# First loads and first products of an attention and MLP-mixer kernel put in another order

## The chip, the cores and the metric

The kernel runs on one core of a Trainium2 chip. The core has a matrix engine (TensorE, PE in the profile), a vector engine (VectorE, DVE), a scalar engine (ScalarE, ACT), a general engine (GpSimd, POOL) and a sync engine (SyncE, SP). Each runs its own list of instructions in order, and they wait for each other by semaphores. SP, ACT and POOL also issue DMAs, which 16 DMA engines carry out. The metric is the device time of one execution in microseconds (us), smaller being better.

## What is computed

Eight batches of attention with eight heads, with no softmax but a division by the root mean square, and then an MLP mixer on the result:

```
kv  = einsum('bhsd,bhse->bhde', k, v)             # 8 x 8 heads, seq 576, head_dim 64
o   = einsum('bhsd,bhde->bhse', q, kv)
x   = o / sqrt(mean(o*o, -1) + 1e-6) * g_norm     # heads side by side: (8, 576, 512)
h   = relu(x.transpose(0,2,1) @ w_tok1) @ w_tok2  # token mixing, 576 -> 256 -> 576
u   = x + h.transpose(0,2,1)
out = u + relu(u @ w_ch1) @ w_ch2                 # channel mixing, 512 -> 1536 -> 512
```

Everything is float32. The weights reach the chip as 64-bit words and are turned into float32 on ACT and DVE.

## The kernel before

**Tiles.** The 576 rows of a batch are cut into 4 tiles of 128 rows (512 rows, `LO`) and a remainder of 64 rows (`HF`). k and v of a batch lie in tiles `k_in`, `v_in` of 128 partitions by 5 slots of 512: slots 0 to 3 hold the main rows (4 consecutive rows to a partition, 1024 KB in all) and slot 4 holds the remainder in partitions 0 to 63 (128 KB), the other half being zero. There are two such tiles each, for the even and the odd batch. q of a batch comes transposed, as 128 partitions by 4 head pairs by 512 rows (`qT`, 1024 KB), and its last 64 rows in a tile of their own (`qR`).

**Pairs.** Two batches are worked together as a pair, so that the two remainders fill one tile. A pair has nine x tiles: 0 to 3 of its first batch (side 0), 4 to 7 of its second (side 1), and 8 with both remainders. `attention` numbers them by c (0 to 4) and half: c = 0, 1 are the first batch, c = 2, 3 the second, c = 4 the remainders.

**Stages.** In the first 187 us attention and token mixing of four pairs are interleaved on PE; channel mixing follows until the end. The change lies in the first pair's stage, which takes about the first 40 us.

**Order.** The order of work on each engine is the order of the program text, because every instruction is recorded with `keep_in_program_order`. The interleaving of a stage is written out by hand as a list of short names, which `play` calls one after the other. The list for the first pair is `start` (line 1297). In it, with s for a side or batch, c for a pair of x tiles and t for a half:

- `kv s half`: the products of k and v of a batch, for half of its heads, into the PSUM tile `ps_kv` (line 371). For each block it adds up over slots j = 0 to 4, so the remainder is the last term. `e s half` copies the result to `kvp`: on DVE for side 0 of the first pair, else on ACT (line 385).
- `a c t`: q times `kvp` for one x tile, into a PSUM bank `ps_o`, of which there are two (line 393). `a40` is the remainder tile, shown as `ps_r`.
- `q c t`: the square on ACT (L455); `g c t`: times `g_norm` on DVE, which writes the x tile (L451); `t c t`: the sum of squares on DVE (L472); `m`, `r`, `i`: mean (DVE), root (ACT), inverse (DVE, four instructions). Only when both `q` and `g` have read a bank can the next `a` but one use it.
- `d c t`: the x tile scaled by the inverse on DVE, one instruction (L509). `s c t`: the same on ACT, eight instructions of 64 columns (L505).
- `h s t j`: token mixing of x tile j of side s with half t of `w_tok1`, into `ps_h` (line 539); x tiles 0 and 1 use the first block of weights, 2 and 3 the second.
- `w n k`: step k of weight block n (1 and 2 on ACT and DVE: scale; clamp, shift, add). `w0*` and `w1*` are the two blocks of `w_tok1`, `w2*` its remainder, `w3*` and `w4*` `w_tok2`.
- `l`, `lq`, `lr`: loads of k and v, q, and q's remainder, for the batch two further on.
- `j n`: n products of the identity with itself, for a PE that would else stand still.

**Loads ahead of the list.** Lines 1275 to 1283 issue: k and v of batch 0 (k on SP's queue, v on ACT's), q of batch 0, the two blocks of `w_tok1`, k and v of batch 1, q of batch 1, both remainders of q, and the remainder of `w_tok1`. All but v of batch 0 go through SP. ACT then issues `g_sb`, the 64 values of `g_norm` sent to 128 partitions in rows of 256 bytes. The loads use eight semaphores in turn, so each issue first waits until the DMA eight places back has landed.

Of the kernel before, what the change touches and what calls it, by code (L numbers as in the profile page):

```python
# [11 lines left out]
F32 = mybir.dt.float32  # L12
# [8 lines left out]
def kernel(  # L21
# [33 lines left out]
    P = 128  # L55
# [5 lines left out]
    J, JJ, HF = 4, 5, 64  # L61
    LO = P * J
    assert D == 64 and DM == 512 and S == LO + HF and B % 2 == 0
    NC, NF, NTOK = DM // P, DCH // P, DTOK // P
    HP = H // 2
# [7 lines left out]
    T = 2 * P  # L73
# [4 lines left out]
    def pool(name, bufs, side="left", stack=ctx, **kw):  # L78
        return stack.enter_context(tc.tile_pool(name=name, bufs=bufs, side=side,
                                                reuse_waits="tile", **kw))  # L80
# [10 lines left out]
    qtp = pool("qtp", 2, "left", left)  # L91
# [30 lines left out]
    def dma(o, i, engine=nc.sync):  # L122
        keep(engine.dma_start(o, i))  # L123
# [14 lines left out]
    qT, q_rest = {}, {}  # L138

    def load(b):  # L140

        if b >= B:
            return

        queues = (nc.sync, nc.sync if b else nc.scalar)
        for dst, t, e in zip((k_in[b % 2], v_in[b % 2]), (k, v), queues):
            dma(dst[:, :J], t[b, :LO].rearrange("(p j) e -> p j e", j=J), e)
            dma(dst[:HF, J], t[b, LO:], e)

    def load_q(b):  # L150
        if b < B:
            qT[b] = qtp.tile([P, HP, LO], F32, name="qT", tag="qT", bufs=2)
            dma(qT[b], q[b].rearrange("(c p) s -> p c s", p=P)[..., :LO])

    def load_q_rest(b):
        if b < B:
# [57 lines left out]
    def get_tok1(i):  # L214

        rows = words(moe_w_tok1)[:LO].rearrange("(i j p) n w -> i p j n w", j=2, p=P)
        return block(2 * DTOK, lambda raw: [(raw.rearrange("p (j n) w -> p j n w", j=2), rows[i])], w_tok1[i])

    def get_tok1_rem():
        w = words(moe_w_tok1)[LO:]  # L220
        return block(DTOK, lambda raw: [(raw[:HF], w), (raw[HF:], w)], w_tok1r)
# [139 lines left out]
    def attention(pair, groups):  # L361
# [154 lines left out]
        for s in range(2):  # L516
            for h in range(2):
                steps |= {f"kv{s}{h}": do(kv, s, h), f"e{s}{h}": do(evict, s, h),
                          f"l{s}": do(load, 2 * pair + 2 + s)}
            steps |= {f"lq{s}": do(load_q, 2 * pair + 2 + s), f"lr{s}": do(load_q_rest, 2 * pair + 2 + s)}  # L520
# [735 lines left out]
    def play(lines, after={}, **stages):  # L1256
# [3 lines left out]
        for name in " ".join(lines).split():  # L1260
# [5 lines left out]
            else:  # L1266
# [4 lines left out]
    tok1 = [get_tok1(i) for i in range(J // 2)] + [get_tok1_rem()]  # L1271
    tok2 = [get_tok2(t) for t in range(NTOK)]
    channel = ([get_ch1(c, f) for f in range(2) for c in range(NC)]
               + [get_ch2(f) for f in range(NF // 2)])
    load(0)
    load_q(0)
    for block in tok1[:2]:
        block[0]()
    load(1)
    load_q(1)  # L1280
    load_q_rest(0)
    load_q_rest(1)
# [4 lines left out]
    for t in zeroed:  # L1287
# [8 lines left out]

    start = [
        "j14 kv00 e00", "kv01 e01 l0", "a00 g00 q00", "a01 g01 q01 t00 t01 m0 w01",
        "a10 w02 r0 i0 w03 d00 w04 d01 q10 w30 w40 lq0", "a11 q11 g10 g11 w11 j10",
        "h000 h010 w12 w13 w14 t10 t11 m1 r1", "h001 h011", "kv10 e10", "kv11 e11 i1 d10 d11 l1", "a20 q20",  # L1300
        "a21 q21 g20 g21 t20 t21 m2", "h002 h012 r2 i2 d20", "a30 q30 g30", "a31 q31 s21 g31 t30", "h003 h013 t31 m3",
        "a40 q40 r3 i3 d30 s31 g40 t40 m4 r4 w21 i4 s40 lr0 lr1"]
    middle = [
        "h100 h110 h101 h111 w31 w22 w23 w24", "kv00 e00 -lq1 w32 w33 w34",
# [156 lines left out]
```

## Time and profile before

| what | us |
|---|---|
| device time, median of 3 runs (lowest, highest) | 773.03 (772.90, 773.72) |
| device time of the profiled execution | 774.16 |
| its span, first to last instruction | 772.3 |
| PE busy | 761.5 |
| DVE busy | 642.8 |
| ACT busy | 277.5 |

Device time includes 1.9 us around the span. Busy time is what an engine spent in instructions. A timeline row gives start, length, engine, line, operation, output and inputs, number of instructions, and in brackets how long the engine stood idle before it and what released it. On PE every float32 product shows as two records. All products are recorded in one helper (line 135), so rows are told apart by the tile they write. SP's timeline around the first loads:

```profile
0.74 1.01 SPq L123 DMA_DIRECT2D k_in<-in_k_dram  x2
1.80 1.01 SPq L123 DMA_DIRECT2D qT<-in_q_dram  x1
2.86 1.25 SPq L123 DMA_DIRECT2D raw<-in_moe_w_tok_dram  x2
9.08 1.04 SPq L123 DMA_DIRECT2D k_in<-in_k_dram  x2
10.56 0.86 SPq L123 DMA_DIRECT2D v_in<-in_v_dram  x2
13.68 0.38 SPq L123 DMA_DIRECT2D qT<-in_q_dram  x1
```

Here the gap between 4.1 and 9.08 is the wait for a semaphore of the eight: the first MB of v landed at 9.04.

### The profile page before, as it was taken

What the parts mean: (1) busy time and instruction counts of PE and PEld (TensorE: products, weight loads), DVE (VectorE), ACT (ScalarE), POOL (GpSimd) and SP (SyncE); (2) the same over time, 40 slices, a digit from 0 to 9 for tenths busy, and PEclk for the clock granted to TensorE, in tenths of its full rate; (3) what the DMA queues carried; (4) which work ended last, traced back from release to release, by engine and by line L of the source; (5) the groups of instructions that cost most, each with busy time, mean ns of one, the idle gap of its engine ahead of it and who ended that gap; (6) DMA issues with size and microseconds to landing.
All of it is one profiled execution on the core that took longest, in us unless ns stands there. A gap on an engine that the chain in (4) does not pass through costs nothing.

```text
span 772.3 us, 12663 instructions
## 1 busy us (share of the span) xinstructions
PE 761.5 (99%) x4682; PEld 613.5 (79%) x4682; DVE 642.8 (83%) x945; ACT 277.5 (36%) x555; POOL 112.1 (15%) x124
## 2 busy tenths in 40 slices
PE   7999999999999999999999999999999999999998
PEld 6655555545888888888888888888888888888887
DVE  2867887897776868989978889987998997798996
ACT  2376575765210233521134252223352224325221
POOL 1002021113410000002240001042000218000204
PEclk9999999999999999999999999999999999999999
DMA  8999999499799696598898577999659879955679
GB/s 309 323 343 362 372 374 359 174 289 346 245 279 357 258 300 188 167 279 184 232 228 266 148 215 230 249 192 266 197 159 281 174 217 208 207 150 152 150 203 119
DMA packets 137819, 188.29 MB, mean 244 GB/s; under 512 B 48800, under 2 KB 95392, under 8 KB 135712
## 3 DMA queue, kind: packets, MB, share of 16 engines
q1 hardware_dynamic: 101744, 167.54, 69.1%
q0 software_dynamic: 34816, 18.36, 16.0%
q10 hardware_dynamic: 1200, 1.61, 0.6%
q8 instruction: 37, 0.61, 0.3%
q14 instruction: 22, 0.18, 0.1%
HBM read 138.31 MB, written 49.15 MB: 243 GB/s over the span
## 4 chain that ended last, share of the span: by engine, by line
PE 95%; DMA 3%; DVE 1%; SPq 0%; ACT 0%; issue 0%; ACTq 0%
PE ps_d L135 28%; PE ps_b L135 19%; PE ps_a L135 19%; PE ps_u L135 8%; PE ps_h L135 7%; PE ps_v L135 5%; DMA qT<-in_q_dram 3%; PE ps_c L135 3%; PE ps_w L135 2%; PE ps_o L135 2%; PE ps_kv L135 2%; PE ps_r L135 0%; DVE x L451 0%; DVE ms L472 0%; SPq L123 0%
## 5 line engine op out<-in xcount | busy, mean ns | idle before, releaser
L135 PE MATMUL ps_d<-ui,w 128*128 128x256 f32 x504 | 118.6, 379 | 0.0
L135 PEld LDWEIGHTS ps_d<-ui,w 128*128 128x128 f32 x504 | 95.8, 190 | 13.0
L132 ACT COPY ps_d<-ps_a 128x768 f32<-128x768 f32 (+1 forms) x56 | 32.0, 572 | 199.9 <-PE ps_a L135 196.9
L126 DVE TENSOR_TENSOR v<-v,v 128x1536 f32<-128x1536 f32 (+2 forms) x70 | 103.3, 1483 | 0.3
L135 PE MATMUL ps_b<-sv,w 128*128 128x256 f32 x324 | 78.9, 379 | 0.0
L135 PE MATMUL ps_a<-v,w 128*128 128x256 f32 x324 | 78.8, 379 | 0.0
L1205 POOL DMA_DIRECT2D out_dram<-us x24 | 26.7, 1834 | 291.9 <-ACT p L132 286.2
L135 PEld LDWEIGHTS ps_b<-sv,w 128*128 128x128 f32 x324 | 61.2, 190 | 8.9 <-issue 0.6
L135 PEld LDWEIGHTS ps_a<-v,w 128*128 128x128 f32 x324 | 61.6, 190 | 8.4
L135 PE MATMUL ps_u<-h,w_tok 128*128 128x512 f32 (+1 forms) x160 | 64.7, 599 | 0.0
L135 PE MATMUL ps_d<-v,w 128*128 128x256 f32 x258 | 62.7, 379 | 0.0
L129 ACT ACTIVATE v<-v 128x768 f32<-128x768 f32 (+1 forms) x54 | 42.7, 822 | 55.1 <-DVE v L126 53.4
L135 PE MATMUL ps_h<-x,w_tok 128*128 128x512 f32 x128 | 57.4, 599 | 0.3 <-DVE w_tok L188 0.3
L1205 POOL DMA_DIRECT2D out_dram<-r x40 | 41.3, 1927 | 102.0 <-ACT p L132 80.3
L135 PE MATMUL ps_d<-sv,w 128*128 128x256 f32 x228 | 55.4, 379 | 0.0
L135 PEld LDWEIGHTS ps_d<-v,w 128*128 128x128 f32 x258 | 48.9, 190 | 6.6
L135 PEld LDWEIGHTS ps_u<-h,w_tok 128*128 128x128 f32 (+1 forms) x160 | 25.6, 179 | 31.1 <-issue 26.7
L135 PEld LDWEIGHTS ps_d<-sv,w 128*128 128x128 f32 x228 | 43.3, 190 | 5.9
L135 PE MATMUL ps_a<-uT,w 128*128 128x256 f32 x192 | 46.7, 379 | 0.0
L135 PEld LDWEIGHTS ps_h<-x,w_tok 128*128 128x128 f32 x128 | 23.5, 190 | 27.7 <-issue 25.0
L135 PE MATMUL ps_b<-ui,w 128*128 128x256 f32 x168 | 40.8, 379 | 0.0
L135 PEld LDWEIGHTS ps_a<-uT,w 128*128 128x128 f32 x192 | 36.5, 190 | 5.0
(165 smaller groups left out, 1292.4 us busy)
## 6 DMA issues: line engine op xcount, KB each, us to landing
w<-parts SPq DMA_DIRECT2D x168, 384.0 KB, 3.8
w<-parts SPq DMA_DIRECT2D x56, 192.0 KB, 3.8
uT<-blocks SPq DMA_DIRECT2D x36, 256.0 KB, 5.5
k_in<-in_k_dram SPq DMA_DIRECT2D x8, 1024.0 KB, 12.2
qT<-in_q_dram SPq DMA_DIRECT2D x8, 1024.0 KB, 12.6
out_dram<-x POOLq DMA_DIRECT2D x16, 512.0 KB, 8.0
v_in<-in_v_dram SPq DMA_DIRECT2D x7, 1024.0 KB, 15.8
raw<-in_moe_w_ch_dram SPq DMA_DIRECT2D x8, 768.0 KB, 11.5
```

What stands on the lines that cost most here:

```text
L126: keep(engine.tensor_tensor(out=o, in0=a, in1=b, op=op))
L129: keep(nc.scalar.activation(o, a, AF.Relu))
L132: keep(nc.scalar.copy(o, a))
L135: keep(nc.tensor.matmul(*a, **kw))
L1205: keep(nc.gpsimd.dma_start(to, t()[ds(b * Q, Q), at].rearrange("p n l j -> p n (l j)"), accum_op=ALU.add))
```

## The change

There are four edits. In `load`, the remainder of k and of v is issued ahead of the main rows, for every batch. `load_q` can load a range of q's rows, and batch 0's q is loaded as rows 0 to 255, then the first block of `w_tok1`, then rows 256 to 511, then the second block; later batches load q whole as before. In `start`, x tile 1 (c = 0, half 1) is scaled by ACT (`s01`, after `q11`) where DVE did it (`d01`). And PE's order in the second half of `start` is another: `h002 h012` stand ahead of `a20 a21` instead of behind them, and `h003 h013` ahead of `a30 a31`; the steps of the inverse move along in the list. The numbers of instructions on PE and POOL stay the same; DVE has one less, ACT eight more, and SP one more DMA.

```diff
         queues = (nc.sync, nc.sync if b else nc.scalar)
         for dst, t, e in zip((k_in[b % 2], v_in[b % 2]), (k, v), queues):
+            dma(dst[:HF, J], t[b, LO:], e)
             dma(dst[:, :J], t[b, :LO].rearrange("(p j) e -> p j e", j=J), e)
-            dma(dst[:HF, J], t[b, LO:], e)
-
-    def load_q(b):
+
+    def load_q(b, at=slice(0, LO)):
         if b < B:
-            qT[b] = qtp.tile([P, HP, LO], F32, name="qT", tag="qT", bufs=2)
-            dma(qT[b], q[b].rearrange("(c p) s -> p c s", p=P)[..., :LO])
+            if at.start == 0:
+                qT[b] = qtp.tile([P, HP, LO], F32, name="qT", tag="qT", bufs=2)
+            dma(qT[b][..., at], q[b].rearrange("(c p) s -> p c s", p=P)[..., at])
...
     load(0)
-    load_q(0)
-    for block in tok1[:2]:
+    for i, block in enumerate(tok1[:2]):
+        load_q(0, slice(i * T, i * T + T))
         block[0]()
     load(1)
...
     start = [
         "j14 kv00 e00", "kv01 e01 l0", "a00 g00 q00", "a01 g01 q01 t00 t01 m0 w01",
-        "a10 w02 r0 i0 w03 d00 w04 d01 q10 w30 w40 lq0", "a11 q11 g10 g11 w11 j10",
-        "h000 h010 w12 w13 w14 t10 t11 m1 r1", "h001 h011", "kv10 e10", "kv11 e11 i1 d10 d11 l1", "a20 q20",
-        "a21 q21 g20 g21 t20 t21 m2", "h002 h012 r2 i2 d20", "a30 q30 g30", "a31 q31 s21 g31 t30", "h003 h013 t31 m3",
+        "a10 w02 r0 i0 w03 d00 w04 q10 w30 w40 lq0", "a11 q11 s01 g10 g11 w11 j10",
+        "h000 h010 w12 w13 w14 t10 t11 m1 r1", "h001 h011", "kv10 e10", "kv11 e11 i1 d10 d11 l1", "h002 h012",
+        "a20 q20", "a21 q21 g20 g21 t20 t21 m2", "h003 h013 r2 i2 d20", "a30 q30 g30", "a31 q31 s21 g31 t30 t31 m3",
         "a40 q40 r3 i3 d30 s31 g40 t40 m4 r4 w21 i4 s40 lr0 lr1"]
```

## The prediction

> **What bounds the kernel now.** I read the page first (busy shares), then PE's waits, then PE's timeline of the first 45 us, the chain of waits for the same stretch, the DMA issues one by one, and the windows of the DMA dip near 9 us.
>
> ```profile
> PE 761.5 (99%) x4682; PEld 613.5 (79%) x4682; DVE 642.8 (83%) x945; ACT 277.5 (36%) x555; POOL 112.1 (15%) x124
> PE ps_j L135 <- POOL ident masks.py:199: 3.3, 1, 3.3
> PE ps_o L135 <- DMA qT<-in_q_dram: 2.2, 2, 1.1
> PE ps_o L135 <- ACT sq L455: 0.5, 1, 0.5
> PE ps_kv L135 <- DMA v_in<-in_v_dram: 0.4, 1, 0.4
> PE ps_h L135 <- DVE w_tok L188: 0.3, 1, 0.3
> PE ps_r L135 <- DVE x L451: 0.2, 1, 0.2
> ```
>
> These are all the waits that PE has in the whole execution (total, times, longest, in us). They all lie before 36 us. From there to its last matmul PE never waits, so whatever moves `a40` (the ps_r matmuls) moves the end by as much. Apart from the fixed 3.3 us at the start, 3.7 us of waiting is all that a reordering of this stage could remove, and a later `a40` is lost in full.
>
> ```profile
> 13.80 2.02 PE L135 MATMUL ps_o<-kvp,qT 128*128 128x128 f32 x16 [1.12 <-DMA qT<-in_q_dram]
> 20.95 3.70 PE L135 MATMUL ps_h<-x,w_tok 128*128 128x512 f32 x8 [0.32 <-DVE w_tok L188]
> 24.61 2.76 PE L135 MATMUL ps_kv<-v_in,k_in 128*64 128x64 f32 x80
> 28.47 2.02 PE L135 MATMUL ps_o<-kvp,qT 128*128 128x128 f32 x16 [1.10 <-DMA qT<-in_q_dram]
> 30.33 1.88 PE L135 MATMUL ps_h<-x,w_tok 128*128 128x512 f32 x4
> 35.93 1.09 PE L135 MATMUL ps_r<-kvp,qR 128*64 128x128 f32 x16 [0.22 <-DVE x L451]
> ```
>
> These rows of PE's timeline (start, length) are `a00`/`a01`; `h000` to `h011`; `kv10`/`kv11`; `a20`/`a21`; `h002`/`h012`; `a40`. The row without a wait, 24.61, matters most: it shows none, yet it has hardly any slack:
>
> ```profile
> v_in<-in_v_dram SPq DMA_DIRECT2D x1, 1024.0 KB, 13.9
> v_in<-in_v_dram SPq DMA_DIRECT2D x1, 128.0 KB, 14.2
> ```
>
> These are batch 1's v, main rows and remainder (KB, us from issue to landing). SP issued them at 10.56 and 10.95, so they landed at 24.5 and about 25.15. `kv10` starts at 24.61, 0.1 us after the main rows, and its first remainder product (after 16 of the 80 records, 0.55 us in) comes at 25.16. Before, the order main-then-remainder let PE work through the main rows while the remainder was still on its way.
>
> ```profile
> 8.00:9.00 1.00, 1.00 (x6) 1.00 (x6) 0.00 (x0) 0.00 (x0) 0.00 (x0) 1.00 1.09 229
> 9.00:10.00 1.00, 1.00 (x20) 0.87 (x18) 0.00 (x0) 0.00 (x0) 0.00 (x0) 1.00 0.78 127
> 10.00:11.00 1.00, 0.60 (x22) 0.47 (x18) 0.00 (x0) 0.00 (x0) 0.00 (x0) 1.00 0.63 205
> 11.00:12.00 1.00, 1.00 (x42) 1.00 (x40) 0.42 (x1) 0.00 (x0) 0.00 (x0) 1.00 1.03 397
> ```
>
> The last column is GB/s. Between 8 and 11 us the remainders and the 256-byte rows of `g_sb` are in service and the rate falls from about 410 to 127-229; everything behind them on the one SP queue lands later for it.
>
> [...] k (SP) and v (ACT), 1 MB each, issued together at 0.74, took 8.1 and 8.3 us. [...] while `g_sb`'s rows from ACT's queue are served, q behind SP's queue moves at a third of its rate. [...] In the trace's landings of v's main rows, 15 of 16 engines were done at 23.0 and the last at 24.47. So a wait on a whole DMA costs the slowest engine's time. [...] Here gaps of up to 1.12 us left it at 1.000; no row shows a longer one after the start.
>
> **The change part by part.**
>
> Remainders first, batch 0. All of k and v have to be there before `kv00`. Before, it started at 9.51 on the main rows, stalled 0.40 and ended at 12.67. Their bytes are the same, and the first two microseconds run slow anyway (0, 66 and 164 GB/s in the windows 0-1, 1-2 and 2-3 us), so the two 128 KB pieces should mostly fit into that ramp. Then the main rows land at 9.2 to 9.8 instead of 8.8 to 9.1. `j14` holds PE until 9.5 in any case. So `kv01` ends at 12.3 to 12.8: a gain of 0 to 0.4.
>
> q in halves. `a00` and `a01` need only q's first half. It was q as a whole that landed at 13.66, while kvp was copied by 13.14. The half is issued with 512 pieces of 1 KB instead of rows of 2 KB. In the packet records a 1 KB packet of other loads takes 46 ns and a 2 KB packet 84, so the whole q costs 16 engines 64 x 46 - 32 x 84 = 256 ns more each. I take the landing at 12.0 to 13.3, and `a00` at 12.9 to 13.4: 0.4 to 0.9 earlier. The chain from there to `h000` (gain, square, sum, root, scale, and the decode of block 0, which lands before q's second half now) has no other DMA in it and shifts along. q's second half lands near 15 to 15.8; `a10` needs it at 15.4 to 15.9, so that is nearly free, at worst 0.3.
>
> Scaling by ScalarE. 8 activations in 2.02 us (the ACT row at 34.58) replace one DVE instruction of 0.69. They run from about 19.45 to 21.5. `h001` needs them at 22.8: nothing. Block 1's decode starts on ACT 2.2 us later, at 21.5 instead of 19.26. DVE reaches it at 22.2 anyway, having lost the 0.69, so its chain to the scaled tile of `h002` ends at 27.2 instead of 27.6. If the cover went, `h002` would be late, but it now runs at 27.4 at the earliest. Cost 0.
>
> Remainder first, batch 1: here is the new wait. `kv10` can't start before the last piece of batch 1 is in, and this is now the 1 MB of v. It has the same place in the queue that the remainder had, 25.14, plus D, the delay of the whole stream. So PE starts at 25.14 + D + 0.1 = 25.24 + D, not at 24.61 and not at the 23.7 to 24.2 that the earlier `a00` would allow. Behind it on PE stand `kv11` and everything else; the gain of the first steps is swallowed.
>
> PE reordered. `kv10`/`kv11` take 2.76. Then `h002 h012` fill the gap in which `a20` waited 1.10 for q: 1.72 (30.33 to the next start at 32.05). So `a20` starts at 25.24 + D + 4.48 = 29.72 + D instead of 28.47; q of batch 1, 28.33 before, is there. From `a20` to `a40` it isn't PE that decides. The chain of waits runs `a20`, square, gain, two sums, root, inverse, scale, the gain that frees the bank, `a40`: 35.93 - 28.47 = 7.46 us, all on ACT and DVE, in unchanged order. PE has only 1.95 + 1.8 + 1.95 us of work in it. Before, it had a second pair of `h` products to put in there and waited 0.22; now one pair has been spent earlier and the wait grows to about 1.8. So `a40` = 29.72 + D + 7.46 = 37.18 + D, against 35.93: +1.25 + D. Even without the DMA wait (24.61 for `kv10`), the reordering alone costs 4.48 + 7.46 - 11.32 = 0.62.
>
> SP's queue: one more DMA shifts which earlier DMA each issue waits for. Now v of batch 1 waits for q's first half (about 13, before 10.5), q of batch 1 for `g_sb` (11.7). More than 1 MB stands in the queue all that time, so it doesn't run dry: 0. Remainders first in later batches: v of batch 2 landed at 37.3 and 38.0 and is used at 40.58, later ones have more room: 0.
>
> The unknown is D. Low end: all loss between 8 and 11 us goes (3 x 410 - 561 = 669 KB, 1.6 us), less the 0.26 of the smaller packets: -1.3. High end: [...] 0.26 for the packets and 0.4 of the remainders not hidden in the ramp: +1.2. I take +0.5: `g_sb` still goes out behind v and holds up q as before[...].
>
> The sum: 1.25 + 0.5 = +1.75 us. The profiled execution has a span of 772.3 in 774.16; the span would become 774.05. On the median of the runs shown, 773.03, that is 774.8.
>
> **Rivals.**
>
> *The DMA does not get slower* (D from -0.8 to 0.3): `kv10` starts at 24.5 to 25.5 and the total is +0.45 to +1.55, around 774.0. For it: the ramp at the start has room. [...]
>
> *The other side, not slower:* the remainders and `g_sb` no longer meet, and the stream runs 0.8 to 1.3 us ahead. At D = -1.3 v of batch 1 lands for a `kv10` at 23.94, just about where the earlier `a00` lets PE be (23.7 to 24.2); the gain of the first steps is then worth 0.67 and pays for the 0.62 of the reordering: 1.25 - 1.3 = -0.05, 773.0. It decides from D = -0.8, where +0.45 is left. For it: the 669 KB lost between 8 and 11 us. Against: `g_sb` is still there.
>
> *Heavier:* D over 1.0, with q's second half late for `a10` too: +2.25 to +3.2, about 775.8. [...] PE's clock is a small part of this: its longest gap grows to 1.8 us, and each us at a lower clock would show in the windows.
>
> **How the numbers follow.** Forecast (D 0.3 to 1.0) 0.50; DMA not slower 0.30; other side 0.08; heavier 0.12. What can be told from no change is 0.2%, 1.55 us here. The forecast's middle is just past it, so slower is 0.50 + 0.12 = 0.62; same 0.36, the second case and the third; faster 0.02, since nothing in the working reaches -1.55. The range 773.0 to 776.1 runs from the lower edge of the second case to the middle of the heavier one and leaves out about 0.13.
>
> **What would show it.** Right: PE's row of `kv10` has a wait for v of 0.5 to 2 us; `a00` starts near 13; the row of ps_r waits 1.5 to 2 us for the gain on DVE, and 7.4 to 7.5 us lie between `a20` and `a40`; PE has no waits after it. Wrong: `kv10` with no wait, `a40` before 36.5, or a wait in later batches.

## The result, and the profile after

| | before | after |
|---|---|---|
| device time, median of 9 runs each (lowest, highest), us | 773.35 (772.90, 774.54) | 775.14 (774.89, 778.92) |
| ratio to before, 95% interval | | 1.0033 (1.0018 to 1.0048) |
| span of the profiled execution, us | 772.3 | 772.9 |

The median became 1.8 us longer. In a second set of 21 runs the ratio was 1.0022 (1.0013 to 1.0032). But the profiled execution's span grew by only 0.6. The spans of the nine runs explain part of the difference: five lie between 772.4 and 772.9 with a mean granted clock of 1.000, four between 774.3 and 775.3 with 0.996 or 0.998. So there are two effects, one in every run and one in about half of them. A third part lies outside the spans: four of the nine runs, the median one among them, took 2.5 to 3.6 us outside their span, where 1.9 to 2.1 is usual. Some runs of most of the other kernels, of the one before too, did the same, and no run tells why.

PE's waits after the change (total, times, longest, in us):

```profile
PE ps_j L135 <- POOL ident masks.py:199: 3.3, 1, 3.3
PE ps_r L135 <- DVE x L452: 1.9, 1, 1.9
PE ps_kv L135 <- DMA k_in<-in_k_dram: 1.1, 1, 1.1
PE ps_kv L135 <- DMA v_in<-in_v_dram: 0.9, 1, 0.9
PE ps_o L135 <- ACT sq L456: 0.5, 1, 0.5
PE ps_h L135 <- DVE w_tok L189: 0.3, 1, 0.3
```

The two waits of `a00` and `a20` for q, 2.2 us together, are gone. In their place stand 1.1 us for k ahead of `kv00`, 0.9 us for v ahead of `kv10`, and 1.9 us ahead of `a40`, where 0.2 had been. PE's timeline after the change shows them in place:

```profile
10.78 2.55 PE L135 MATMUL ps_kv<-v_in,k_in 128*64 128x64 f32 x80 [1.14 <-DMA k_in<-in_k_dram]
13.26 2.19 PE L135 MATMUL ps_o<-kvp,qT 128*128 128x128 f32 x16
20.57 3.70 PE L135 MATMUL ps_h<-x,w_tok 128*128 128x512 f32 x8 [0.31 <-DVE w_tok L189]
25.22 2.55 PE L135 MATMUL ps_kv<-v_in,k_in 128*64 128x64 f32 x80 [0.95 <-DMA v_in<-in_v_dram]
27.70 1.98 PE L135 MATMUL ps_h<-x,w_tok 128*128 128x512 f32 x4
29.52 1.95 PE L135 MATMUL ps_o<-kvp,qT 128*128 128x128 f32 x16
36.91 1.09 PE L135 MATMUL ps_r<-kvp,qR 128*64 128x128 f32 x16 [1.93 <-DVE x L452]
```

`a00` came 0.54 earlier (13.26), `h000` 0.38 earlier (20.57), and `kv10` 0.61 later. `a40` starts at 36.91, 0.98 later than before. From there PE has no listed wait. The end moved by 0.6 and not 0.98, because in the second pair the remainder products, which took 1.05 us with a hole of 0.31 us in their records, now took 0.69; the first row is of the kernel before, the second of the one after:

```profile
63.39 1.05 PE L135 MATMUL ps_r<-kvp,qR 64*64 64x64 f32 x32
64.36 0.69 PE L135 MATMUL ps_r<-kvp,qR 64*64 64x64 f32 x32
```

No run tells why the hole was there; the waits listed for the kernel before do not show it.

### The profile page after: what moved, and what is told of

It reads as the page before. It is cut to its first block, busy times and chain, and to the rows that moved or that the text cites. A ratio compares the mean times of both kernels' runs of the same rounds, so it can differ in the third digit from the quotient of the medians.

```text
span 772.9 us, 12669 instructions
## 1 busy us (share of the span) xinstructions
PE 761.0 (98%) x4682; PEld 613.4 (79%) x4682; DVE 642.0 (83%) x944; ACT 279.3 (36%) x563; POOL 112.1 (15%) x124
## 4 chain that ended last, share of the span: by engine, by line
PE 96%; DMA 3%; DVE 1%; SPq 0%; ACT 0%; issue 0%; ACTq 0%
PE ps_d L135 28%; PE ps_b L135 19%; PE ps_a L135 19%; PE ps_u L135 8%; PE ps_h L135 8%; PE ps_v L135 5%; PE ps_c L135 3%; PE ps_kv L135 2%; PE ps_w L135 2%; PE ps_o L135 2%; DMA v_in<-in_v_dram 2%; DMA qT<-in_q_dram 1%; PE ps_r L135 0%; SPq L123 0%; DVE x L452 0%; DVE ms L473 0%
## 5 line engine op out<-in xcount | busy, mean ns | idle before, releaser
L135 PEld LDWEIGHTS ps_h<-x,w_tok 128*128 128x128 f32 x128 | 23.5, 190 | 27.7 <-issue 24.8
```

What stands on the lines that cost most here:

```text
L135: keep(nc.tensor.matmul(*a, **kw))
```

## The experiments

Each was timed beside the kernel before on its chip. In the diffs the sign shows the step from the kernel that is named. Line numbers of the changed kernels differ by one or more from those before. "Spans" are those of all timed runs of a kernel, not of the profiled one alone.

### Each edit alone, and all but one

PE's new order alone, from the kernel before:

```diff
-"kv11 e11 i1 d10 d11 l1", "a20 q20",
-"a21 q21 g20 g21 t20 t21 m2", "h002 h012 r2 i2 d20", "a30 q30 g30", "a31 q31 s21 g31 t30", "h003 h013 t31 m3",
+"kv11 e11 i1 d10 d11 l1", "h002 h012",
+"a20 q20", "a21 q21 g20 g21 t20 t21 m2", "h003 h013 r2 i2 d20", "a30 q30 g30", "a31 q31 s21 g31 t30 t31 m3",
```

> The kernel before with PE's new order alone (h002 h012 ahead of a20, h003 h013 ahead of a30). Theory 1 (the wait of a40 on DVE is the main cost, and the late v of batch 1 only adds to it): kv10 stays at 24.6 with no wait, h002 starts at about 27.65 when its x tile is scaled, a20 at 29.5 instead of 28.47, a40 waits 1.7 to 2 us and starts near 36.9 instead of 35.93; span +0.6 to +1.0. Theory 2 (the order costs nothing, the late v of batch 1 is all): a40 at 36.0, span within 0.2 of before. Theory 3 (TensorE's clock: longer gaps let it fall in part of the runs): some runs show a clock under 1.000 here, where those of before do not.

Measured: 1.0023 (1.0017 to 1.0030). Three rows of its PE timeline:

```profile
25.01 2.72 PE L135 MATMUL ps_kv<-v_in,k_in 128*64 128x64 f32 x80 [0.39 <-DMA v_in<-in_v_dram]
27.69 1.98 PE L135 MATMUL ps_h<-x,w_tok 128*128 128x512 f32 x4
36.90 1.10 PE L135 MATMUL ps_r<-kvp,qR 128*64 128x128 f32 x16 [1.93 <-DVE x L451]
```

`a40` starts at 36.90 and waits 1.93, just as after the whole change. The order does that with no other edit: `h002` starts at 27.69, when `kv11` is done and its x tile, scaled at 27.6, has just come; `a20` follows 1.82 later where it would have started at 28.5, and DVE's chain behind `a20` takes its 7.4 us. Its runs also fall into two groups: twelve spans from 772.7 to 773.6, and nine from 774.4 to 775.0 with a clock of 0.998; the 50 runs of the kernel before beside it have none over 773.0. In these windows of the profiled run, which is of the second group, the third figure from the end is PE's granted clock:

```profile
38.00:39.00 1.00, 1.00 (x2) 0.49 (x3) 0.80 (x3) 0.73 (x2) 0.00 (x0) 0.57 1.00 343
39.00:40.00 1.00, 1.00 (x2) 0.42 (x2) 0.78 (x4) 0.08 (x1) 0.00 (x0) 0.50 1.02 391
40.00:41.00 1.00, 1.00 (x2) 0.34 (x1) 0.96 (x3) 0.89 (x4) 0.00 (x0) 0.50 1.04 387
41.00:42.00 1.00, 1.00 (x3) 0.45 (x2) 1.00 (x2) 1.00 (x5) 0.00 (x0) 0.72 1.14 424
```

From 38.15, 1.2 us after the wait ended, PE ran at half clock for 3.41 us; the eight products behind `a40`, which take 3.70 us in the profile after, took 5.40 here. That is the second effect: 1.7 us in this run.

Remainders first alone, for every batch, from the kernel before:

```diff
+            dma(dst[:HF, J], t[b, LO:], e)
             dma(dst[:, :J], t[b, :LO].rearrange("(p j) e -> p j e", j=J), e)
-            dma(dst[:HF, J], t[b, LO:], e)
```

> The kernel before with remainders first alone. Theory 1: kv10 waits for v of batch 1 and starts at 25.1 to 25.4, but kv11 then ends near 27.8 and a20 still waits for q until 28.4, so the lateness is swallowed by the wait that was there: a40 at 35.9 to 36.2, span +0 to +0.3. Theory 2 (the late v is the whole cost): a40 late by 0.6 to 1.0 and the span too. kv00 should wait for k until about 10.7, as after the whole change.

Measured: 0.9991 (0.9984 to 0.9997). Its PE timeline:

```profile
24.93 2.55 PE L135 MATMUL ps_kv<-v_in,k_in 128*64 128x64 f32 x80
28.47 2.02 PE L135 MATMUL ps_o<-kvp,qT 128*128 128x128 f32 x16 [0.99 <-DMA qT<-in_q_dram]
35.93 1.09 PE L135 MATMUL ps_r<-kvp,qR 128*64 128x128 f32 x16 [0.21 <-DVE x L451]
```

`a20` and `a40` stand at 28.47 and 35.93, the very times of before: a `kv10` that is 0.3 late runs into the wait for q that was there anyway. So this lateness costs nothing while PE's order is the old one; all but the order, below, tests the same with a longer wait for v. (`kv00` started at 9.44 and not near 10.7, as was expected: k had landed at 9.30.)

q in halves and x tile 1 scaled by ACT, from the kernel before (`load_q` as in the change):

```diff
-    load_q(0)
-    for block in tok1[:2]:
+    for i, block in enumerate(tok1[:2]):
+        load_q(0, slice(i * T, i * T + T))
         block[0]()
...
-... w03 d00 w04 d01 q10 w30 w40 lq0", "a11 q11 g10 g11 w11 j10",
+... w03 d00 w04 q10 w30 w40 lq0", "a11 q11 s01 g10 g11 w11 j10",
```

> The kernel before with q in halves and x tile 1 scaled by ACT, main rows first and PE's order as before. Theory 1: a00 starts at 13.2 to 13.4 (0.4 to 0.6 earlier), kv10 at about 24.6 on v's main rows, and a20 at the landing of batch 1's q, which is 0 to 0.3 later than 28.33; a40 at 35.9 to 36.2, span within 0.3 of before. If the 1 KB packets cost more than the 0.26 worked out, q of batch 1 lands after 28.8 and the span shows it.

Measured: 1.0008 (1.0000 to 1.0016). `h000` started at 20.10, 0.85 earlier than before, but `kv10` then waited 1.03 for v until 24.82, and `a40` stood at 36.01. The gain is there and is swallowed at the next load.

The whole change with the main rows first again (diff: the one of the remainders, undone):

> The whole change but for the remainders, which stand behind the main rows as before. Theory 1: kv10 at 24.2 to 24.8 instead of 25.22, a20 near 28.9 instead of 29.52, a40 still waits 1.7 to 2 us and starts at 36.2 to 36.5; span +0.2 to +0.4 against before, so about half of the change's cost goes. Theory 2: all of it goes, a40 at 35.9. Theory 3: the gaps of PE are as long as with the whole change, so part of the runs shows a clock under 1.000.

Measured: 1.0038 (1.0024 to 1.0051), from six runs. Two rows of its PE timeline:

```profile
24.49 2.76 PE L135 MATMUL ps_kv<-v_in,k_in 128*64 128x64 f32 x80 [0.36 <-DMA v_in<-in_v_dram]
36.39 1.09 PE L135 MATMUL ps_r<-kvp,qR 128*64 128x128 f32 x16 [1.93 <-DVE x L452]
```

In these two profiles, then, the late v did cost 36.91 - 36.39 = 0.52 of `a40` with the new order. The landings scatter: in the next section's profile, with remainders first as well, `kv10` starts at 24.96 and not at 25.22. The time didn't fall: four of the six runs have a mean clock of 0.998, and two took 3.2 and 4.6 us outside their span.

The whole change with PE's order as before (diff: the one of the order, undone):

> The whole change but for PE's order, which is as before. Theory 1 (the order is the cost, now that it alone gave a40 at 36.90): kv10 still waits for v of batch 1 until about 25.2, a20 waits for q until about 28.4, a40 near 35.95 with a wait of about 0.2, no half-clock stretch in the records; time within 0.1% of before. Theory 2 (remainders first cost as much by themselves when a00 is earlier): a40 at 36.5 or later.

Measured: 0.9997 (0.9989 to 1.0005). Its PE timeline:

```profile
24.98 2.55 PE L135 MATMUL ps_kv<-v_in,k_in 128*64 128x64 f32 x80 [0.94 <-DMA v_in<-in_v_dram]
28.14 2.02 PE L135 MATMUL ps_o<-kvp,qT 128*128 128x128 f32 x16 [0.60 <-DMA qT<-in_q_dram]
35.59 1.09 PE L135 MATMUL ps_r<-kvp,qR 128*64 128x128 f32 x16 [0.21 <-DVE x L452]
```

The wait for v is as long as with the whole change, and yet all of the loss is gone. Theory 2 falls: PE's order is what costs. Two of the 13 runs have a clock of 0.997 and 0.998 with spans of 772.7 and 771.7, so a low mean clock alone does not make a run long.

### Is it the wait that lowers the clock?

The whole change, with seven products of the identity put into the wait ahead of `a40`; their results are not used:

```diff
+    def fill_gap(n):
+        o = ps["kv"].tile([P, 2, P], F32, name="ps_y", tag="kv")
+        for _ in range(n):
+            matmul(o[:, 0], lhsT=ident, rhs=ident, start=True, stop=True)
...
+    more["y7"] = do(fill_gap, 7)
...
-        "a40 q40 r3 i3 ...
+        "y7 a40 q40 r3 i3 ...
```

> The whole change with seven products of the identity put into PE's wait ahead of a40 (1.7 us of PE time in a wait of 1.93, their results unused). Theory 3 (the long wait lets TensorE's clock fall in part of the runs): a40 stays at 36.9 to 37.0, no run has the half-clock stretch of 3.4 us near 38 us, all spans are 772.4 to 773.2 and none is at 774 or above; the time falls by 0.5 to 1 us against the whole change on average. Rival (the clock falls for another reason, such as the gaps near 10 and 25 us, or by chance): about half of the runs still have spans above 774.

Measured: 1.0012 (1.0005 to 1.0019). Its PE timeline:

```profile
34.55 1.73 PE L135 MATMUL ps_y<-ident 128*128 128x128 f32 x14
36.66 1.09 PE L135 MATMUL ps_r<-kvp,qR 128*64 128x128 f32 x16 [0.37 <-DVE x L452]
```

PE does 1.73 us more work and the long spans are all but gone: 20 of 21 lie between 772.3 and 773.6, and none has a clock under 0.999. One span, 775.5, has no such mark and stays unexplained. What is left of the loss, 0.12% or 0.9 us, fits the late `a40`, which at 36.66 is nearly as late as before the filling (36.91).

For comparison the unfilled change once more, on another chip:

> The whole change once more, to see how often TensorE's clock falls in it, beside the version with the gap filled (1.0012 of before, 1 of 21 spans at 774 or above). Theory 3 (the long wait ahead of a40 lets the clock fall in part of the runs): of the runs, a third to two thirds have a span of 774 or above with a clock under 1.000, the others 772.4 to 773.6; ratio to before 1.002 to 1.003, above that of the filled version. Rival (the four slow runs of nine were chance or that chip): at most 1 in 10 at 774 or above, ratio 1.001.

Measured: 1.0022 (1.0013 to 1.0032); ten of 21 runs have spans from 771.8 to 773.3, eleven have 773.8 to 776.3 with a clock of 0.998 or less. The two intervals overlap (up to 1.0019 filled, from 1.0013 unfilled); it is the count, one long span of 21 against eleven, that tells the two apart. The half clock is no mark of one chip, since it also stands in the records of the order alone, on a third chip, and of a later kernel on a fourth; but filled and unfilled were not run on the same one. In the profiled run of these eleven the half clock stands elsewhere:

```profile
17.46 3.50 PE L135 MATMUL ps_o<-kvp,qT 128*128 128x128 f32 x16 [2.58 <-ACT root L483]
```

```profile
17.00:18.00 1.00, 0.54 (x4) 0.57 (x5) 0.93 (x5) 0.44 (x2) 0.00 (x0) 0.87 0.90 356
18.00:19.00 1.00, 1.00 (x6) 1.00 (x6) 0.96 (x4) 0.00 (x0) 0.00 (x0) 0.50 1.01 367
19.00:20.00 1.00, 1.00 (x7) 1.00 (x6) 0.98 (x3) 0.60 (x1) 0.00 (x0) 0.50 1.16 285
```

Here q's second half landed only at 17.33 (one of the 16 DMA engines was 2.3 us behind the others), `a10` waited 2.58 us for it, and the clock fell behind that wait. (The row names ACT's root, which `a10` doesn't read.) So my theory 3 was right on the cause and too narrow on the place: waits of 1.93, 2.58 and 2.24 us ahead of `a40`, `a10` and `kv00` (the last in a profile below) were each followed by the half clock.

The clock changes in one run's records lie whole multiples of 3.413 us apart: a half clock lasted 3.413 in all three profiles, and full clock before it 3.413, 10.240 and 30.720; in the profiles of the kernel before and of the whole change, full clock lasted 764.585, which is 224 times 3.413. So I laid a grid of 3.413 us through the changes of each profile, taking its points as the times at which the clock could have changed; that is a reading, since most points show no change. It lies differently in different profiles: half clock begins at 38.15 (order alone), 17.74 (second set) and 11.02 us (other bank), full clock at 9.36 (before) and 9.47 (whole change). Set against it, the long waits of six profiles sort themselves (worked out from the clock records and PE's timelines):

```
profile              wait of PE      part of it in one 3.41-us step   clock in the step after
order alone          34.97 - 36.90   1.93                             half
change, second set   14.88 - 17.46   2.58                             half
other bank (below)    8.75 - 10.99   2.24                             half
whole change         34.98 - 36.91   1.80                             full
all but remainders   34.46 - 36.39   1.69                             full
all but order         8.16 - 10.54   1.63                             full
```

On these six, a step with 1.93 us or more of standing still was followed by one at half clock, and one with 1.80 or less was not. Two more long waits agree: that of `a40` in the second set's profile (36.56 - 38.49, 1.66 us of it in one step) and that of `a00` with the remainders first alone (11.99 - 14.15, 1.46) were followed by full clock. My estimate, if the grid lies anywhere with equal chance, which was not shown: a wait of 1.93 falls whole within a step in (3.41 - 1.93) / 3.41 = 43% of the runs; 9 of 21, 43%, had the low clock with the order alone.

### Does `a40` wait for its bank or for its data?

The whole change, with the remainder tile's bank taken from the pool in which the sums of kv stood:

```diff
-            o = ps["o"].tile([P, DM], F32, name="ps_r", tag="o")
+            o = ps["kv"].tile([P, DM], F32, name="ps_r", tag="kv")
```

> The whole change with a40 writing into a bank of the other pool (where the sums of kv stood, free by then), so that it need not wait until DVE has read a30. Theory 1 (what is lost is that a40 has to wait for DVE behind a20, because its bank is a30's): the ps_r row starts at 34.9 to 35.1 with no wait; the next products (h100) wait 0.1 to 0.4 for the x tile scaled by DVE and start near 36.3, where the whole change had 37.93 and the kernel before 36.95; no half-clock stretch; spans near 771.5, about 0.6 below before. Rival (DVE's chain behind a20 is the bound, whatever bank a40 has): h100 near 37.9 and no gain.

Measured: 0.9994 (0.9986 to 1.0002), median span 771.5 against 772.2. Its PE timeline:

```profile
10.99 4.10 PE L135 MATMUL ps_kv<-v_in,k_in 128*64 128x64 f32 x80 [2.24 <-DMA k_in<-in_k_dram]
35.77 1.09 PE L135 MATMUL ps_r<-kvp,qR 128*64 128x128 f32 x16
37.17 3.70 PE L135 MATMUL ps_h<-x,w_tok 128*128 128x512 f32 x8 [0.31 <-DVE x L510]
```

`a40` no longer waits, and `h100` waits 0.31 for its x tile. This profile has the half clock at 11 us (kv took 4.10 instead of 2.55), which makes its early rows 1.5 us late; even so `h100` is 0.8 earlier than with the whole change. So `a40` waited for its bank; what bounds `h100` now is its x tile, the end of DVE's chain. The same with main rows first:

> As the last, with main rows ahead of the remainders. Theory 1, with kv10 on v's main rows at 24.5: a40 at 34.4 to 34.6, h100 at 35.8 to 36.0, span 0.3 to 0.5 below the last. If remainders first are better for PE's 2.55 instead of 2.76 us of kv10 and kv11, the two are within 0.2.

Measured: 0.9997 (0.9989 to 1.0005), median span 771.15. `h100` starts at 36.07, with `kv10` at 24.78 after 1.20 of waiting for v. The two can't be told apart by their ratios, nor either of them from the kernel before.

### What holds the loads up between 8 and 11 us?

`g_norm` as one row, spread by a product with ones, from the kernel before:

```diff
-    dma(g_sb, ... 128 rows of 256 bytes, all read from g_norm ..., nc.scalar)
+    keep(nc.gpsimd.memset(g_row, 0.0))
+    keep(nc.gpsimd.memset(ones, 1.0))
+    dma(g_row[:1], ... one row of 256 bytes ..., nc.scalar)
+    def spread():
+        o = ps["o"].tile([P, DM], F32, name="ps_g", tag="o")
+        matmul(o[:, :D], lhsT=ones, rhs=g_row, start=True, stop=True)
+        keep(nc.vector.tensor_copy(g_sb[:, 0], o[:, :D]))
...
-"kv01 e01 l0"
+"kv01 e01 gs l0"
```

> The kernel before with g_norm loaded as one row of 256 bytes and sent to the 128 partitions by one product with ones and one copy, in place of 128 rows read from the same place. If these reads make the dip of the DMA rate at 8 to 11 us: the windows 9-10 and 10-11 rise from 127 and 205 GB/s to over 350, q lands at 12.2 to 12.6 instead of 13.66, v of batch 1 near 23.3, its q near 27.1; a20 starts at 27.8 to 28.0 when kvp is copied, a40 at 35.2 to 35.4, span -0.4 to -0.8. If the remainders make the dip: rates as before, everything within 0.2 of before.

Measured: 1.0005 (0.9997 to 1.0013). The windows of this kernel (last two figures: busy share of the DMA engines, GB/s):

```profile
8.00:9.00 1.00, 1.00 (x8) 1.00 (x7) 0.00 (x0) 0.00 (x0) 0.00 (x0) 1.00 1.05 215
9.00:10.00 1.00, 0.61 (x16) 0.45 (x16) 0.00 (x0) 0.00 (x0) 0.00 (x0) 1.00 1.07 148
10.00:11.00 1.00, 0.30 (x11) 0.16 (x6) 0.00 (x0) 0.00 (x0) 0.00 (x0) 1.00 0.98 262
```

The dip stays, with engines that are busy all the time: with main rows first it does not come from `g_norm` alone, since the rates of 9 to 11 us rose only from 127 and 205 GB/s to 148 and 262. With q in halves and the scaling by ACT besides:

> As the last, with q in halves and x tile 1 scaled by ACT, main rows first, PE's order as before. If the reads of g_norm make the dip: q's first half lands near 11, a00 starts at 12.6 to 12.9 when kvp is copied, kv10 at 23.5 to 23.8, a20 at the landing of q near 27.3, a40 at 34.8, span -1.0 to -1.3: the earlier a00 is worth something once the stream is ahead. If not: as the kernel with q in halves and the scaling alone, +0 to +0.3.

Measured: 1.0005 (0.9999 to 1.0012). The same dip; and the one row, behind v on ACT's queue, was issued only at 9.45, and PE waited 1.12 us for it ahead of `a00`.

With remainders first the picture differs. These are windows of the whole change:

```profile
7.00:8.00 1.00, 1.00 (x7) 1.00 (x7) 0.00 (x0) 0.00 (x0) 0.00 (x0) 1.00 0.83 270
8.00:9.00 1.00, 1.00 (x6) 1.00 (x6) 0.00 (x0) 0.00 (x0) 0.00 (x0) 1.00 0.64 203
9.00:10.00 1.00, 0.64 (x4) 0.39 (x2) 0.00 (x0) 0.00 (x0) 0.00 (x0) 1.00 0.49 167
```

The engines are idle part of the time, and no remainder is in service: batch 0's had landed by 4.27. So the whole change, with the other bank, and the one row issued by POOL:

> As the kernel with the other bank and remainders first, with g_norm loaded as one row on POOL's queue and sent to the partitions by a product. With remainders first the dip of the DMA rate stood at 7 to 10 us, when no remainder was in service and engines were idle part of the time, so g_norm's 128 reads should be its cause here: k of batch 0 lands at 9.0 to 9.5 instead of 10.64, kv00 starts at 9.6, the windows 7-8, 8-9 and 9-10 show over 350 GB/s, v of batch 1 lands near 24.0 and its q near 27.0; h100 at 35.3 to 35.8. If the dip has another cause (k behind v of another queue): k lands at 10.4 to 10.7 all the same and the windows stay at 170 to 270.

Measured: 0.9968 (0.9956 to 0.9980), 771.26 against 774.11: 2.8 us below the kernel before, and all five spans between 769.2 and 769.4. Its windows and PE timeline:

```profile
8.00:9.00 1.00, 1.00 (x8) 1.00 (x7) 0.00 (x0) 0.00 (x0) 0.00 (x0) 1.00 0.93 348
9.00:10.00 1.00, 0.94 (x26) 0.78 (x26) 0.00 (x0) 0.00 (x0) 0.00 (x0) 1.00 1.11 374
10.00:11.00 1.00, 1.00 (x42) 1.00 (x39) 0.26 (x1) 0.00 (x0) 0.00 (x0) 1.00 1.06 382
```

```profile
9.32 2.55 PE L135 MATMUL ps_kv<-v_in,k_in 128*64 128x64 f32 x80
22.82 2.55 PE L135 MATMUL ps_kv<-v_in,k_in 128*64 128x64 f32 x80
34.03 3.70 PE L135 MATMUL ps_h<-x,w_tok 128*128 128x512 f32 x8 [0.31 <-DVE x L510]
```

The dip is gone, k landed at 9.18 instead of 10.64, q of batch 1 at 25.45 instead of 28.27, no wait of PE behind its start is over 0.52, and `h100` starts at 34.03 where the kernel before had 36.95. The landing of k alone would not show it, since it came at 9.30 with the remainders first alone; that of q's first half does, 10.64 against 12.34 to 13.34 in the five profiles with q in halves, remainders first and 128 rows of `g_norm`. In these trials it took both: the remainders early and `g_norm` out of the way. The trials of the one row differ in the issuing queue too, and the last in the bank and PE's order; this was not tried apart.

## Why the prediction was right, and where it was not

The direction, the size (+1.75 forecast, +1.79 measured between the medians) and the range held. That the size fits so closely is luck. The forecast's main case needed the loads to be later by D = 0.3 to 1.0 us, and v of batch 1 was not later at all; what came is the first rival, "The DMA does not get slower", to which I gave 0.30: `a40` 0.98 later, within its +0.45 to +1.55. The rest of the measured difference came from the clock, which I put at almost nothing, and from time outside the spans, which the prediction does not have. The median run after has full clock and a span of 772.6; 2.5 us of its time lie outside.

*`a40` and its wait: right.* The wait of 1.8 was measured as 1.93, the 7.46 us from `a20` to `a40` as 7.39, and the test with the other bank shows its cause. That a later `a40` is lost in full was not quite so in the profiles, because of the hole in the second pair.

*The first steps: half right.* `a00` came in the time given (13.26), but not by the path given: q's first half was in at 12.38, and it was `kv01`, done at 13.33 and not by 12.8, that held PE. `kv00` was expected by 9.8 and came at 10.78, since k's main rows landed at 10.64; v's were in at 7.25. q's second half (15.23) landed in time, and the scaling by ACT cost nothing.

*D, the delay of the stream: wrong.* I took +0.5. v of batch 1 landed at 25.08, which makes D about zero (25.22 against 25.24 + D); in the five other profiles with remainders first and 128 rows of `g_norm` it landed from 24.74 to 25.59. With D = 0 the sum is 1.25, and with `kv` in 2.55 and not 2.76, because it no longer stops halfway, and the smaller differences of the chain, it is the 0.98 measured. The runs with one row of `g_norm` show what stands behind D: two causes of the dip, of which the change removes one, the remainders between main rows and q, and meets the other. So holding `g_sb`'s rows alone to blame for the late q was too simple: with main rows first, the rates of 9 to 11 us rose without them only from 127 and 205 GB/s to 148 and 262. About 0.5 of the 1.2 at the high end of D was my estimate of what they cost q's smaller packets. In the kernel before, 42 packets of SP's queue stand beside 41 of ACT's from 9.5 to 10.2 us, but 70 beside 36 from 10.2 to 10.9, so an even exchange was shown only for the first stretch. And what `kv10` waited for was mostly one DMA engine: 15 of the 16 had their part of v in by 23.85, the last at 25.08.

*The wait for v as the main cost: half right.* The wait is there (0.95) and swallows the gain of `a00`, as forecast. But alone it costs nothing; with the new order it costs 0.52, and the order costs 0.97 without it. The two are not a sum: `h002` stood at 27.7 with either. The 0.62 that I gave the order alone took `kv10` at 24.61 and let `h002` follow it at once. In the run of the order alone v landed 0.4 later, and an earlier `kv10` would have gained little, as the x tile of `h002` is scaled only at 27.6 when DVE scales tile 1 too.

*TensorE's clock: this step failed.* I put a wait of 1.8 us at almost nothing. That was my estimate: the longest gap behind the start that the kernel before shows is 1.12 us, at a clock of 1.000. A wait of 1.93 us that falls within one step of the 3.413-us grid brought half clock for the next 3.413, in the profile of the order alone. In the sets with this wait unfilled, about half of the runs had the low clock and were 1.1 to 2.1 us longer than the rest, and filling the wait took nearly all of them away. Of the 0.33% measured at first, 2.5 us between the means, I estimate from the spans about 0.7 for the late `a40` (772.7 in the five runs at full clock, 772.0 in the other sets of the kernel before), 0.9 for the clock (2.1 us in four of nine runs) and 0.4 for the time outside the spans; the remaining 0.5 is open, the mean of the kernel before being 0.3 to 0.6 lower in this set than in the others.

## What to carry to other kernels

Before products are moved into a wait, ask what will stand in the place they leave: here a wait of 1.10 us on a load was exchanged for one of 1.93 on a chain of small VectorE and ScalarE steps, and the remedy was another bank. Read the spans and the granted clock of every run, not of the profiled one alone, because a wait of PE can cost something after its end too, in a part of the runs: behind the 1.93 us ahead of `a40`, eight products took 5.40 us in the profile of the order alone and 3.70 in that of the whole change. And where a gain at the start disappears, follow it to the next load: here the only version that was faster than the kernel before by more than about 0.1% is the one that also took the small broadcast out of the way.

## What the runs showed of the hardware

- Waits of PE of 1.93, 2.24 and 2.58 us, each within one step of the grid of 3.413 us, were followed by half clock for 3.413 us (order alone, other bank, second set of the change). A wait of 1.93 us of which 1.80 lay in one step (whole change) was followed by full clock.
- 128 rows of 256 bytes, all read from one place, went through at 24 to 32 rows per us from 6 to 10 us (whole change). Beside them 18 to 32 rows of 8 KB per us started from 7 to 10 us, where it had been 50 from 5 to 6, with the engines partly idle (0.49 to 0.83 busy).
- After the two remainders the 1 MB loads of k and v, on two queues, were not served alike in six of seven profiles, but landed 1.0 to 4.1 us apart: v at 7.25 and k at 10.64 in one, k at 6.93 and v at 9.72 in another of the same kernel. In the seventh, with the remainders first alone, it was 0.2. With main rows first they landed about 0.3 us apart or less.
- While the remainders, loads to 64 partitions, were in service in the middle of the stream, the engines were busy and the rate low: 229 GB/s at a share of 1.09 (kernel before, window 8 to 9), and 148 to 262 at 0.98 to 1.07 (kernel before with one row, windows 8 to 11), where full loads ran at 410 to 418 (kernel before, windows 4 to 7). The cause was not looked for.
